# Band loads of 24 rows instead of 23 in a kernel of four attention layers

## The chip, the cores and the metric

The kernel runs on one core of a Trainium2 chip, as one program with one launch. The metric is the device time of that program in microseconds (us), the median of several runs. Times of single instructions come from one execution that the hardware profiler recorded.

## The reference, cut to what matters

Four layers of attention follow one another on 2048 tokens of 512 features with 32 heads of 16 features, each with a layer norm ahead and a residual behind:

```
x = A_x
x = x + _A_ref(_layernorm(x), A_wqkv, A_wo)   # dilated: token s sees s, s-2, ..., s-14
x = x + _B_ref(_layernorm(x), B_wqkv, B_wo)   # block: token s sees the last 256 tokens
x = x + _A_ref(_layernorm(x), A_wqkv, A_wo)
x = x + _B_ref(_layernorm(x), B_wqkv, B_wo)
```

The change is in layer A. There a query has eight keys, of its own parity (even or odd position): `logits = einsum("bhsd,bhswd->bhsw", q, kg) * scale`, a softmax over the eight, and `o = einsum("bhsw,bhswd->bhsd", attn, vg)`.

## The kernel before, in words

The sequence is cut into 8 chunks of 256 tokens, and the two pairs of layers run over them one after the other: for each pair of layers and each chunk first layer A (`layer_a`), then layer B (`layer_b`). That makes 16 chunks. All steps are given to a planner (`Plan`) as tasks with an engine, a cost and the values that they read and write. A table of numbers (`ORDER`) sets the order of each engine's tasks; the planner merges the five engines' rows by its costs, and so decides which buffers and PSUM banks a task gets. Steps of layer B of one chunk lie between steps of layer A of the next one. All but a few DMAs are issued by SP (SyncE), in the order of its row: an issue that must wait holds up all that stands behind it.

Layer A splits a chunk by parity into two halves of 128 tokens (`t` = 0 and 1). For each half TensorE (PE) computes scores in windows (L1171), ACT copies them out, and DMAs by way of DRAM bring the eight scores of each query into one row (`sd`, `l`). VectorE (DVE), ACT and GpSimd (POOL) make the softmax of them (L1212 to L1229), and L1223 writes the weights into `bands`, spread so that the two tokens of a pair stand side by side.

To weigh the values with them, PE needs the weights transposed: keys on the partitions. That is done by two DMAs through a DRAM tensor `ptd`, one for each half. `put` (L1256) writes `bands` with a stride that moves each query pair two rows down, so that a diagonal band arises; `ptd` is filled with zeros at the start, and `put` always writes the same places. `get` (L1263) reads the band back into `ptt`, an SBUF tile of 128 partitions that is set to zero once (L770), and of which there is only one. `get` issues four DMAs: `bb` = 0 and 1 are two groups of partitions from 0 and from 64, each with 39 keys (`WIN` = 39) for 32 queries; `e` = 0 and 1 are the first and the second eight query pairs of a group. One such DMA is a rectangle: so many rows (keys, on the partitions) by two blocks (`b2`) by 16 x 32 numbers of 4 bytes, which is 2 KB in one piece. The two rectangles of a group begin 16 rows apart and have 23 rows each: keys 0 to 22 and 16 to 38.

`window` (L1251) loads the values of the same keys from DRAM into `vs`: for each `bb` 39 rows by two blocks by 512 numbers, 2 KB in one piece too.

`mix` (L1280) then multiplies: two tasks of 64 matmuls for each half, each matmul with 39 keys in the contraction, alternately for `bb` = 0 and `bb` = 1. The matmuls of `bb` = 0 need the first pair of the four DMAs, those of `bb` = 1 the second. Since `ptt` exists once, the load of half 1 is issued only when the mix of half 0 is done. After the mix DVE picks the right one of two columns (`pick`, L1285), ACT and DVE split the result into two float16 parts (L1079, L1080), and PE multiplies it by the output weights (L1045, L1047, L1048).

Layer B has its scores in L1391 and L1542, with operands that DMAs bring by way of DRAM (`re`, `stk`), the row maxima in L1406, exponentials in L1552 and L1564, and the values in L1597. At its end the sums of the softmax go through `rc` and `scr` (L1660 to L1675) and are multiplied into the output `oc` (L1683).

Of the kernel before, what the change touches and what calls it, by code (L numbers as in the profile page):

```python
# [21 lines left out]
H = 32  # L22
# [5 lines left out]
WIN = 32 + HALO  # L28
# [628 lines left out]
def kernel(  # L657
# [10 lines left out]
    nc = tc.nc  # L668
# [9 lines left out]
    def buf(name, shape, dtype, tag, label, cap=None, group=0):  # L678
        p, n = pools[name]
        return Buf(p, cap or n, shape, dtype, tag, label, group)  # L680
# [43 lines left out]
    ptt = cst.tile([P, 2, 16, H, 2], F32, name="ptt")  # L724
# [391 lines left out]
    def layer_a(l, c):  # L1116
# [127 lines left out]
        for t in range(2):  # L1244
            vs = buf("pvs", [P, 2, D], F32, "vs", f"vs{l}_{c}_{t}")
            vvs = Val(vs)

            def window(t=t, vs=vs):
                x = vd[l][t]
                for bb in range(2):  # L1250
                    nc.sync.dma_start(vs.t[64 * bb : 64 * bb + WIN],  # L1251
                                      bass.AP(tensor=x.tensor, offset=x.offset + (c * P + 64 * bb) * D, ap=[[D, WIN], [32 * D, 2], [1, D]]))

            def put(t=t):
                x = ptd[t]
                nc.sync.dma_start(bass.AP(tensor=x.tensor, offset=x.offset, ap=[[130 * H, 64], [64 * H, WIN_], [1, 2 * H]]),  # L1256
                                  bands[64 * t : 64 * t + 64].rearrange("p k s u -> p k (s u)"))

            def get(t=t):
                x = ptd[t]  # L1260
                for bb in range(2):
                    for e in range(2):
                        nc.sync.dma_start(ptt[64 * bb + 16 * e : 64 * bb + 16 * e + WIN - 16, :, 8 * e : 8 * e + 8].rearrange("p a q s u -> p a (q s u)"),  # L1263
                                          bass.AP(tensor=x.tensor, offset=x.offset + (2 * bb * 65 * 32 + 16 * e * 65) * H, ap=[[64 * H, WIN - 16], [65 * H * 32, 2], [1, 16 * H]]))

            plan.add("SP", 0.8, window, r=[vvd[l, t, c], vvd[l, t, c - 1]], w=[vvs], size=560)
            plan.add("SP", 0.4, put, r=[ve], w=[vptd[t]], size=310)
            plan.add("SP", 1.65, get, r=[vptd[t]], w=[vptt], size=700)
            acc = Banks(psum, 2, [P, 2, 512])
            va, vpk = Val(acc), Val(acc)  # L1270
            accs.append(acc)
            vacc.append([vpk])

            def mix(m0, acc=acc, vs=vs):
                for m in range(m0, m0 + 2):
                    for b2 in range(2):
                        for r in range(4):
                            for bb in range(2):
                                k = slice(64 * bb, 64 * bb + WIN)
                                nc.tensor.matmul(acc.t[32 * r : 32 * r + 32, bb].rearrange("p (a x q u) -> p a x q u", a=2, q=16, u=2)[:, :, 2 * m + b2],  # L1280
                                                 vs.t[k, b2, 32 * (4 * m + r) : 32 * (4 * m + r) + 32], ptt[k, :, :, 16 * b2 + 4 * m + r],
                                                 start=True, stop=True, tile_position=(64 * bb, 32 * r))

            def pick(acc=acc):
                nc.vector.copy_predicated(acc.t[:, :, 0:C],  # L1285
                                          odd.bitcast(I16)[:, 0:1].unsqueeze(1).broadcast_to([P, 2, C]), acc.t[:, :, C:])

            for m0 in (0, 2):
                plan.add("PE", 0.85, lambda f=mix, m0=m0: f(m0), r=[vvs, vptt], w=[va], mode="V", act=0.5, rec=128)
            plan.add("DVE", 0.6, pick, r=[va, vodd], w=[vpk])  # L1290
# [472 lines left out]
```

## Time and profile before

| | |
|---|---|
| median of 3 runs | 1859.56 us (1859.2 to 1865.65) |
| the profiled execution | 1874.45 us, its span 1872.7 us |
| mean granted PE clock | 0.845 of full speed |
| DVE busy | 863.9 us (46%) |
| ACT busy | 825.9 us (44%) |
| POOL busy | 404.9 us (22%) |
| DMA | 183570 packets, 194.67 MB, mean 104 GB/s |

Busy time is the time in which an engine has an instruction under way; issuing a DMA and waiting do not count. A row of a group names line, engine, operation, output and inputs by the program's names, the count, then busy time and the mean of one in ns, then the engine's idle time just before these instructions and what ended most of it. In the timeline a row has start, length, engine (SPq is SP's queue of DMA issues), line and count, and in brackets the idle time ahead of it with what ended it. The table by stretches gives for each engine the busy time in a stretch and the count of instructions, then the granted PE clock, the share of time in which the core's 16 DMA engines were busy (their mean), and what they moved in GB/s.

### The profile page before, as it was taken

To read this page: it belongs to the slowest core of one execution; us is meant where nothing else is said; L and a number is where in the kernel's file an instruction comes from. 1 tells how busy PE (TensorE), PEld (TensorE's weight loads), DVE (VectorE), ACT (ScalarE), POOL (GpSimd) and SP (SyncE) were. 2 spreads that over 40 slices of the span, in tenths; PEclk is the share of its full clock that TensorE was granted. 3 is DMA by queue.
4 is the path that set the end of the run, shared out by engine and by line. 5 is a ranking of instruction groups with operands and counts; after the bars stand their busy time and mean duration, and the time that the engine had idled before them with its cause. 6 is when DMAs were issued, how large, how long until landed. Compare 5 with 4: busy or idle time off the path is not lost. (4 is left out here: it accounts for less than half of the span.)

```text
span 1872.7 us, 64356 instructions
## 1 busy us (share of the span) xinstructions
PE 1375.1 (73%) x28126; PEld 895.2 (48%) x28126; DVE 863.9 (46%) x1961; ACT 825.9 (44%) x1299; POOL 404.9 (22%) x856
## 2 busy tenths in 40 slices
PE   9657958678496784967949496784967678497687
PEld 7434636346263552735526263542735345263354
DVE  5413644453355453454624425453453444346366
ACT  7423526345263452634526162542635345253344
POOL 4120202122131211311313021321212222032112
PEclk9868979889797886988869797896978979788788
DMA  8753433626245254433414243344433454424232
GB/s 261 132 89 114 116 77 95 125 75 151 51 116 95 80 151 64 121 86 105 129 53 139 81 115 105 97 125 78 127 83 84 127 91 138 64 72 122 66 95 60
DMA packets 183570, 194.67 MB, mean 104 GB/s; under 512 B 91484, under 2 KB 121948, under 8 KB 183288
## 3 DMA queue, kind: packets, MB, share of 16 engines
q1 hardware_dynamic: 183032, 190.30, 40.7%
q8 instruction: 220, 3.60, 0.9%
q14 instruction: 62, 0.51, 0.1%
q10 hardware_dynamic: 256, 0.26, 0.1%
HBM read 93.59 MB, written 79.36 MB: 92 GB/s over the span
## 5 line engine op out<-in xcount | busy, mean ns | idle before, releaser
L1280 PE MATMUL banks<-ptt,vs 39*32 39x64 f32 x4096 | 77.8, 305 | 385.5 <-DMA ptt<-ptd 265.2
L1406 DVE TENSOR_REDUCE m<-banks 128x2 f32<-128x512 f32 x448 | 301.4, 688 | 8.2
L1552 ACT ACTIVATE p<-banks,sclB 128x896 f32<-128x896 f32 x224 | 220.7, 1005 | 84.2 <-PE banks L1542 73.5
L1280 PEld LDWEIGHTS banks<-ptt,vs 39*32 39x32 f32 x4096 | 63.7, 143 | 394.5 <-issue 367.7
L1410 DVE COPY_PREDICATED banks<-trm,banks 128x128 f32<-128x128 int16 x448 | 124.3, 291 | 170.1 <-PE banks L1391 163.0
L1079 ACT CAST oh<-banks 128x512 f16<-128x512 f32 x32 | 18.8, 587 | 415.4 <-DVE banks L1285 415.4
L1581 POOL TENSOR_SCALAR_AFFINE_SELECT p<-p 64x256 f32<-64x256 f32 x300 | 122.7, 431 | 347.0 <-ACT p L1552 333.1
L1285 DVE COPY_PREDICATED banks<-odd,banks 128x512 f32<-128x512 int16 x32 | 22.3, 696 | 377.1 <-PE banks L1280 377.0
L1581 POOL TENSOR_SCALAR_AFFINE_SELECT ps<-ps 64x256 f32<-64x256 f32 x292 | 115.8, 418 | 359.5 <-ACT ps L1564 354.4
L1391 PE MATMUL banks<-stk,stk 48*64 48x128 f16 (+3 forms) x3584 | 145.0, 253 | 45.6 <-DMA stk<-re 21.7
L1391 PEld LDWEIGHTS <-stk 48*64 48x64 f16 x3584 | 83.1, 113 | 123.6 <-issue 93.7
L1542 PE MATMUL banks<-stk,stk 64*64 64x192 f16 (+3 forms) x3584 | 124.4, 250 | 22.2 <-DVE m L1406 6.2
L1597 PE MATMUL banks<-p,v 64*32 64x256 f32 (+1 forms) x3584 | 131.5, 399 | 3.6 <-DVE p L1575 1.3
L1564 ACT ACTIVATE ps<-banks,sclB 128x768 f32<-128x768 f32 x112 | 100.1, 900 | 42.4 <-PE banks L1542 33.2
L1542 PEld LDWEIGHTS <-stk 64*64 64x64 f16 x3584 | 74.7, 113 | 74.7 <-issue 62.1
L1180 ACT COPY s<-banks 128x624 f32<-128x624 f32 x64 | 74.5, 1263 | 66.0 <-DMA sd<-s 42.9
L1312 DVE SCALAR_TENSOR_TENSOR el<-banks,eh 128x512 f16<-128x512 f32 x64 | 42.6, 688 | 114.5 <-ACT eh L1309 75.7
L1597 PEld LDWEIGHTS banks<-p,v 64*32 64x32 f32 x3584 | 68.5, 116 | 49.0 <-issue 26.3
L1683 POOL TENSOR_TENSOR oc<-oc,os 128x512 f32<-128x512 f32 x23 | 29.5, 1292 | 245.0 <-DMA os<-scr 75.1
L1614 ACT COPY os<-banks 128x256 f32<-128x256 f32 x112 | 41.4, 372 | 85.8 <-PE banks L1597 83.5
L1597 PE MATMUL banks<-ps,v 64*32 64x64 f32 (+1 forms) x3584 | 76.3, 264 | 3.7 <-issue 3.7
L1597 PEld LDWEIGHTS banks<-ps,v 64*32 64x32 f32 x3584 | 69.6, 114 | 16.0 <-issue 10.0
(216 smaller groups left out, 3245.1 us busy)
## 6 DMA issues: line engine op xcount, KB each, us to landing
stk<-re SPq DMA_DIRECT2D x256, 96.0 KB
sd<-s SPq DMA_DIRECT2D x128, 156.0 KB
re<-eh SPq DMA_DIRECT2D x128, 128.0 KB
ptt<-ptd SPq DMA_DIRECT2D x128, 92.0 KB
vs<-vd SPq DMA_DIRECT2D x64, 156.0 KB
vd<-ve SPq DMA_DIRECT2D x32, 256.0 KB
xm<-y SPq DMA_DIRECT2D x32, 256.0 KB
re<-el SPq DMA_DIRECT2D x64, 128.0 KB
```

Source lines behind the costliest of these rows:

```text
L1180: nc.scalar.copy(S_.t.rearrange("p k (s r) -> p r s k", r=4)[:, 2 * i : 2 * i + 2], pbs[i].t[:, :, 0 : 8 * WIN].rearrange("p r (s k) -> p ...
L1280: nc.tensor.matmul(acc.t[32 * r : 32 * r + 32, bb].rearrange("p (a x q u) -> p a x q u", a=2, q=16, u=2)[:, :, 2 * m + b2], vs.t[k, b2, 32 ...
L1312: nc.vector.scalar_tensor_tensor(e["l"].t[:, :, mp], ps[mp].t, QS, e["h"].t[:, :, mp], op0=ALU.mult, op1=ALU.subtract)
L1391: nc.tensor.matmul(o, lhs, k, start=True, stop=True, tile_position=(64 * par, 64 * h))
L1406: nc.vector.tensor_reduce(out=m.t[:, :, u, qb], in_=ps.t[:, :, 0 : 2 * P], op=ALU.max, axis=AX.X)
L1410: nc.vector.copy_predicated(t[:, :, 0:64], trm[:, 0].bitcast(I16).unsqueeze(1).broadcast_to([P, 2, 64]), t[:, :, C : C + 64])
L1542: nc.tensor.matmul(ps.t[64 * h : 64 * h + 64, par, at + x0 : at + x0 + q1 - q0], stk[hf, kt][r, col, k0 : k0 + 64], stk[hf, 0][r, col, q0: ...
L1552: nc.scalar.activation(big.t[:, 2 * i : 2 * i + 2], ps.t[:, :, 0:448], AF.Exp, scale=scl["B", 1])
L1564: nc.scalar.activation(small.t.rearrange("p (i m) x -> p m i x", i=2), ps.t[:, :, 0:384].rearrange("p m (i x) -> p m i x", i=2), AF.Exp, s ...
L1581: E.affine_select(out=v, in_=v, pattern=[[0, 4], [a, 64]], compare_op=op, fill=0.0, base=0, channel_multiplier=-a)
L1597: nc.tensor.matmul(acc.t[32 * mm : 32 * mm + 32, h, q0:q1], vv[r, blk, 17 * hd : 17 * hd + 32], x.t[r, mm, x0 : x0 + q1 - q0], start=begin ...
L1614: plan.add("ACT", 0.3, lambda acc=acc, some=some: nc.scalar.copy(some(), acc.t[:, 0, 0:C]), r=[vacc], w=[vhf])
```

## The change

The four rectangles of `get` have 24 rows instead of 23, and the two of a group begin 15 rows apart instead of 16: keys 0 to 23 and 15 to 38. The source address moves with it: the second rectangle begins 15 rows and eight pairs on, where it began 16 rows and eight pairs on. The keys that a group covers, 0 to 38, and the tile stay the same; the row added to each rectangle holds zeros of `ptd` outside the band. Tasks, costs, the order of every engine and the waits are the same as before; in SP's row 128 DMAs have another shape, 24x2x512 for 23x2x512.

```
             def get(t=t):
                 x = ptd[t]
                 for bb in range(2):
                     for e in range(2):
-                        nc.sync.dma_start(ptt[64 * bb + 16 * e : 64 * bb + 16 * e + WIN - 16, :, 8 * e : 8 * e + 8].rearrange("p a q s u -> p a (q s u)"),
-                                          bass.AP(tensor=x.tensor, offset=x.offset + (2 * bb * 65 * 32 + 16 * e * 65) * H, ap=[[64 * H, WIN - 16], [65 * H * 32, 2], [1, 16 * H]]))
+                        nc.sync.dma_start(ptt[64 * bb + 15 * e : 64 * bb + 15 * e + 24, :, 8 * e : 8 * e + 8].rearrange("p a q s u -> p a (q s u)"),
+                                          bass.AP(tensor=x.tensor, offset=x.offset + (2 * bb * 65 * 32 + 15 * e * 64 + 16 * e) * H, ap=[[64 * H, 24], [65 * H * 32, 2], [1, 16 * H]]))
```

## The prediction

> **What bounds the kernel now.** I read the page first, then the list of waits, then the timeline around one chunk's two band loads, and last the table by stretches for what the DMA engines do in them. The page has TensorE (PE) busy for 1375.1 of 1872.7 us, so it is without work for 497.6 us. The group table gives each group's idle time, and one group holds most of it:
>
> ```profile
> span 1872.7 us, 64356 instructions
> PE 1375.1 (73%) x28126; PEld 895.2 (48%) x28126; DVE 863.9 (46%) x1961; ACT 825.9 (44%) x1299; POOL 404.9 (22%) x856
> ...
> L1280 PE MATMUL banks<-ptt,vs 39*32 39x64 f32 x4096 | 77.8, 305 | 385.5 <-DMA ptt<-ptd 265.2
> ...
> ptt<-ptd SPq DMA_DIRECT2D x128, 92.0 KB
> ```
>
> L1280 is the mix of the dilated layer: 4096 matmuls are 32 mixes (16 chunks, two token halves) of 128. PE stands still for 385.5 us just before them, 12.0 us a mix; everywhere else it idles 497.6 - 385.5 = 112.1 us in all. The last row is the load that the mix waits for: 128 DMAs of 92.0 KB, four to a mix. The waits name the same cause, or none:
>
> ```profile
> PE banks L1280 <- DMA ptt<-ptd: 265.2, 46, 7.7
> PE banks L1280 <- issue: 84.7, 15, 7.7
> PE banks L1280 <- DMA vs<-vd: 23.0, 3, 12.2
> ```
>
> The 15 waits without a releaser have the same longest value, 7.7 us, as the 46 named ones, so I count them with these. The three on vs are the values' window; where its load stands behind the band load on SP, it is late because of that load. So I take all 385.5 us as the load's.
>
> Then one chunk in the middle. The timeline of SP's queue and that of PE (start, length, what; idle time before it in brackets):
>
> ```profile
> 813.32 5.74 SPq L1263 DMA_DIRECT2D ptt<-ptd  x4
> 819.10 5.69 SPq L1660 DMA_DIRECT2D rc<-os  x4
> ...
> 833.75 0.73 SPq L1251 DMA_DIRECT2D vs<-vd  x2
> 834.58 5.24 SPq L1263 DMA_DIRECT2D ptt<-ptd  x4
> 839.86 5.60 SPq L1665 DMA_DIRECT2D oc<-os  x4
> ```
>
> ```profile
> 824.20 0.39 PE L1280 MATMUL banks<-ptt,vs 39*32 39x64 f32 x2 [5.22 <-DMA ptt<-ptd]
> 831.68 2.04 PE L1280 MATMUL banks<-ptt,vs 39*32 39x64 f32 x126 [7.09 <-DMA ptt<-ptd]
> ...
> 844.86 0.27 PE L1280 MATMUL banks<-ptt,vs 39*32 39x64 f32 x2 [4.03 <-DMA ptt<-ptd]
> ...
> 852.50 2.03 PE L1280 MATMUL banks<-ptt,vs 39*32 39x64 f32 x126 [7.38 <-DMA ptt<-ptd]
> ```
>
> The second load is issued from 834.58. Its first pair of DMAs (partitions 0 to 38) lets two matmuls go at 844.86, 10.3 us later; the second pair lets the other 126 go at 852.50, 17.9 us after the issue. The pairs are 7.64 us apart, and a pair is 2 x 92.0 KB = 188,416 bytes: 24.7 GB/s. The stretches show why so slow:
>
> ```profile
> core 0: us, PE busy (x) PEld busy (x) DVE busy (x) ACT busy (x) POOL busy (x), PEclk, DMA share, GB/s
> 819.50:824.00 4.50, 0.00 (x0) 0.00 (x0) 0.00 (x0) 0.29 (x1) 0.00 (x0) 0.78 0.08 28
> 824.50:831.00 6.50, 0.09 (x1) 0.00 (x0) 0.00 (x0) 0.00 (x0) 0.00 (x0) 0.50 0.33 99
> 834.50:836.00 1.50, 1.50 (x10) 1.16 (x9) 1.44 (x3) 0.57 (x1) 0.00 (x0) 0.62 0.66 199
> 837.00:840.50 3.50, 3.50 (x35) 1.77 (x33) 2.41 (x5) 0.36 (x1) 0.00 (x0) 1.00 0.07 26
> ...
> 845.50:852.40 6.90, 0.00 (x0) 0.00 (x0) 0.00 (x0) 0.00 (x0) 0.00 (x0) 0.53 0.18 45
> ```
>
> From 837.0 to 840.5 little but the band load is under way, and the 16 DMA engines are busy for a share of 0.07 at 26 GB/s. One engine of 16 is a share of 0.0625: the load runs through one engine, its four DMAs one behind the other (4 x 94,208 bytes at 26 GB/s is 14.5 us). Just before, from 834.5 to 836.0, the window loads issued at 833.75 move at 199 GB/s and a share of 0.66. They read the same way, rows of 2 KB in two blocks, and differ in having 39 rows rather than 23. So it is not the row's size, nor HBM, that confines the band load. In 824.5 to 831.0 and 845.5 to 852.4 nothing computes on any engine: the wait is hidden by nothing.
>
> **The change, part by part.** It makes the 128 DMAs of L1263 24 rows instead of 23. No instruction is added, removed or moved on any engine, and no wait is new.
>
> The load's length. The nearest row for a load of the same form that spreads is the window's 199 GB/s: 24 x 2 x 2048 = 98,304 bytes take 0.49 us instead of 3.6 (94,208 at 26 GB/s), four 2.0 us instead of 14.5. The four issues and the time from issue to landing come on top; for these the nearest rows are four unblocked issues on SP, and in the chain of waits a DMA of 144 KB from its issue to what it releases:
>
> ```profile
> 1708.48 2.50 SPq L1660 DMA_DIRECT2D rc<-os  x4
> ```
>
> ```profile
> 1716.68 2.79 DMA ptd<-bands
> ```
>
> The first pair then lands 0.6 + 2.8 = 3.4 us after the load's first issue, the last DMA 1.9 + 2.8 = 4.7 us after it, or 5.3 where it queues a little. When does PE come to the mix? In the rows above at 824.20 - 5.22 = 818.98, which is 5.7 us after the issue at 813.32, and at 844.86 - 4.03 = 840.83, 6.25 us after the issue at 834.58. There nothing of the wait is left. Elsewhere PE comes sooner:
>
> ```profile
> 935.14 2.42 SPq L1263 DMA_DIRECT2D ptt<-ptd  x4
> ```
>
> ```profile
> 945.13 0.39 PE L1280 MATMUL banks<-ptt,vs 39*32 39x64 f32 x2 [6.98 <-DMA ptt<-ptd]
> ```
>
> That is 938.15, 3.0 us after the issue, and about 2 us would stay. I take 1.0 us left per mix, between 0 and 3: 32 us of the 385.5.
>
> [...]
>
> The clock. After a wait of this length PE works at half clock for a while. These are PE's starts after the first mix, then a few later:
>
> ```profile
> 833.83 0.42 PE L1026 MATMUL banks<-xl,wA0h 128*128 128x256 f16 x1
> 834.05 0.42 PE L1027 MATMUL banks<-xh,wA0l 128*128 128x256 f16 x1
> 834.26 0.42 PE L1025 MATMUL banks<-xh,wA1h 128*128 128x256 f16 x1
> ...
> 835.81 0.27 PE L1027 MATMUL banks<-xh,wA1l 128*128 128x256 f16 x1
> 835.92 0.27 PE L1025 MATMUL banks<-xh,wA1h 128*128 128x256 f16 x1
> ```
>
> The same matmuls start every 0.21 us and then every 0.11. Here nine of them, from 833.64 to 835.54, lose 0.95 us. After another mix it lasts longer:
>
> ```profile
> 1162.50:1169.50 7.00, 6.51 (x77) 3.20 (x77) 5.01 (x12) 4.19 (x5) 1.56 (x4) 0.50 0.54 113
> ```
>
> Seven microseconds at 0.50 with PE busy for 6.51 lose up to 3.3. Without the long waits this loss goes too: between 1 and 3 us a mix, and I take 1.5, which is nearer to the row of the first: 48 us.
>
> What comes late instead. Work of other engines that lies in the waits today must find another place. In the stretches above DVE, ACT and POOL do nothing or 0.29 us. A stretch before another mix has more:
>
> ```profile
> 1603.00:1616.00 13.00, 0.39 (x2) 0.18 (x2) 1.88 (x4) 0.00 (x0) 1.47 (x4) 0.66 0.84 35
> ```
>
> DVE's 1.88 us there is the upper end, 32 x 1.88 = 60 us if PE had to wait for all of it; the lower end is 0, and even below it, since the load also holds up what SP issues behind it (rc<-os took 5.69 us to issue where 2.50 is usual, oc<-os 5.60), and DVE waits for one of these:
>
> ```profile
> DVE rc L1669 <- DMA rc<-os: 39.5, 3, 14.5
> ```
>
> I take 30 us of new waits. The two rows added cost 4 KB a DMA in 94 KB; at the window's rate that is 0.02 us a DMA.
>
> The sum, against the profiled execution (1874.45 us with what lies around its span): 1874.45 - 385.5 + 32 - 48 + 30 = 1502.95. That execution stands above the median of the runs by 1874.45 / 1859.56 = 1.008. So 1503 / 1.008 = 1491, rounded **1490 us**.
>
> **The rivals.**
>
> *Slower: the load's time goes by its bytes, whatever its rows.* If something other than the row count confines it to one engine (the overlapping of the two rectangles, the place in DRAM), each DMA carries two packets of 2 KB more at 26 GB/s: 0.16 us, 0.63 for four, 20 us over 32 mixes, 1859.56 + 20 = 1880 us. It decides when the share in such a stretch stays near 0.07. For it: the trace has no load of 24 rows. Against it: the window load, of the same form from the same kind of tensor, is seven times as fast. [...] Chance 0.03; that the compiled load is cut as before, so that nothing changes (1860 us), 0.01.
>
> *Two engines instead of many.* The load would take 7.5 us instead of 14.5 and each mix would win some 7 us, and the half clock would stay: 1859.56 - 32 x 7 = 1636 us. Against it again the window's 0.66. Chance 0.04.
>
> *Another wait takes half of it back.* The chain from a mix to the next layer's output (rc, reciprocal, scr, os, the product at L1683) runs beside the second load today. If PE comes to its product earlier than that chain, it could wait 6 us a chunk and mix: 1490 + 32 x 6 = 1682 us. For it: PE's order is fixed, so one late product stops all behind it. Against it: that chain is late today because its DMAs are issued behind the band load. Chance 0.08.
>
> **How the numbers follow.** The forecast has a chance of 0.84. Its own ends: with nothing left of the wait, 2 us of clock a mix and no new waits, 1874.45 - 385.5 - 64 = 1425, by 1.008 about 1414; with 3 us left a mix, 1 us of clock and 60 us new, 1874.45 - 385.5 + 96 - 32 + 60 = 1613, about 1600. The low end needs three favourable ends at once, and I stop at 1425. 1425 to 1600 leaves out the rivals (0.16) and little of the forecast's own. All but the first rival are faster by far more than 0.5% (about what a measurement of this kernel can tell from no change): faster 0.96, same 0.01, slower 0.03.
>
> **What would show it.** Right: in the changed profile the idle time before L1280 falls from 385.5 to below 100 us, PE's busy share rises from 73% to about 90%, the mean clock from 0.845 to above 0.9, and in the stretch behind a load the DMA share is no longer 0.07 for ten microseconds; SP's four issues of L1263 take about 2.5 us instead of 5. Wrong: if the waits of L1280 on ptt stay at 7 us each, the row count was not the cause; if they go and PE's idle time grows by as much before other lines (L1047 and L1048 behind the product, or L1391 behind stk), the third rival holds; if the clock stays near 0.845 with the waits gone, the 48 us are wrong.

## The result, and the profile after

The changed kernel takes 1471.07 us (median of 4 runs, 1469.52 to 1476.47), the kernel before 1862.61 us on the same chip (1859.2 to 1878.7): a ratio of 0.789, with a 95% interval from 0.7838 to 0.7941. 1490 us were forecast. The profiled execution of the changed kernel took 1476.47 us, its span 1474.8 us, at a mean granted PE clock of 0.949.

The page of the changed kernel, with the rows that answer to those shown of before:

```profile
span 1474.8 us, 64356 instructions
...
PE 1324.0 (90%) x28126; PEld 866.4 (59%) x28126; DVE 866.2 (59%) x1961; ACT 825.8 (56%) x1299; POOL 405.7 (28%) x856
...
L1391 PE MATMUL banks<-stk,stk 48*64 48x128 f16 (+3 forms) x3584 | 144.1, 249 | 51.1 <-DMA stk<-re 26.0
...
L1280 PE MATMUL banks<-ptt,vs 39*32 39x64 f32 x4096 | 59.6, 237 | 24.6 <-issue 12.4
...
ptt<-ptd SPq DMA_DIRECT2D x128, 96.0 KB
```

PE's idle time before the mix fell from 385.5 to 24.6 us. The instructions are the same in number, and DVE, ACT and POOL are busy for the same time as before; only the share of the span has grown. The groups that now wait most on PE are others, L1391 first, but with little more than before (51.1 us, before 45.6 us).

SP's queue around the same chunk as in the prediction, in the changed kernel:

```profile
641.37 2.92 SPq L1263 DMA_DIRECT2D ptt<-ptd  x4
644.33 2.51 SPq L1660 DMA_DIRECT2D rc<-os  x4
...
650.62 0.91 SPq L1251 DMA_DIRECT2D vs<-vd  x2
651.63 1.56 SPq L1263 DMA_DIRECT2D ptt<-ptd  x4
653.23 2.46 SPq L1665 DMA_DIRECT2D oc<-os  x4
```

And PE's mixes there:

```profile
647.26 1.64 PE L1280 MATMUL banks<-ptt,vs 39*32 39x64 f32 x128
...
655.87 0.27 PE L1280 MATMUL banks<-ptt,vs 39*32 39x64 f32 x2 [0.81 <-DVE y L1092]
656.87 1.32 PE L1280 MATMUL banks<-ptt,vs 39*32 39x64 f32 x107 [0.73 <-DMA ptt<-ptd]
```

The first mix runs through without a wait. The second load is issued at 651.63; its first matmul goes 4.2 us later (before: 10.3), and the 0.81 us of wait ahead of it are put down to DVE, no longer to the load. Of the other 126, 107 follow 5.2 us after the issue (before: 17.9), where a wait of 0.73 us on the load ends. The issues behind the loads (rc, oc) take 2.5 us, where before they took 5.69 and 5.60: with the slow load, SP's issues behind it took longer too.

The table by stretches of the changed kernel, across the second load of that chunk:

```profile
core 0: us, PE busy (x) PEld busy (x) DVE busy (x) ACT busy (x) POOL busy (x), PEclk, DMA share, GB/s
...
653.50:655.00 1.50, 1.50 (x8) 0.49 (x5) 1.45 (x3) 0.00 (x0) 0.00 (x0) 1.00 0.69 190
654.50:656.00 1.50, 0.69 (x5) 0.20 (x3) 1.26 (x3) 0.23 (x1) 0.00 (x0) 1.00 0.81 219
```

A share of 0.69 to 0.81 at 190 to 219 GB/s stands where 0.07 and 26 GB/s stood behind the same load (837.00 to 840.50 in the prediction's table). Some of this is other traffic, so the share is not the load's alone.

From all rows of L1263 and L1280 in the two traces one can work out where in a chunk the time went, as means over 16 chunks:

| stretch | before | after |
|---|---|---|
| issue of the first load to the end of its mix | 20.1 us | 7.6 us |
| end of that mix to the issue of the second load | 1.2 us | 2.1 us |
| issue of the second load to the end of its mix | 20.6 us | 8.2 us |
| end of that mix to the next chunk's first load (15) | 68.5 us | 67.6 us |

The first and the third stretch lose 12.4 to 12.5 us a chunk each, 398 us over 16 chunks; the spans differ by 1872.7 - 1474.8 = 397.9 us. The second grows by 0.9 us and the fourth shrinks by as much: all else cancels.

### The profile page after: what moved, and what is told of

Same layout as the page of the kernel before. It is cut to its first block, busy times and chain, and to the rows that moved or that the text cites. A ratio compares the mean times of both kernels' runs of the same rounds, so it can differ in the third digit from the quotient of the medians.

```text
span 1474.8 us, 64356 instructions
## 1 busy us (share of the span) xinstructions
PE 1324.0 (90%) x28126; PEld 866.4 (59%) x28126; DVE 866.2 (59%) x1961; ACT 825.8 (56%) x1299; POOL 405.7 (28%) x856
## 5 line engine op out<-in xcount | busy, mean ns | idle before, releaser
L1391 PE MATMUL banks<-stk,stk 48*64 48x128 f16 (+3 forms) x3584 | 144.1, 249 | 51.1 <-DMA stk<-re 26.0
L1391 PEld LDWEIGHTS <-stk 48*64 48x64 f16 x3584 | 82.0, 111 | 131.8 <-issue 97.3
L1597 PE MATMUL banks<-p,v 64*32 64x256 f32 (+1 forms) x3584 | 120.7, 371 | 6.1 <-issue 3.0
L1597 PEld LDWEIGHTS banks<-p,v 64*32 64x32 f32 x3584 | 64.9, 110 | 45.6 <-issue 24.5
L1611 DVE TENSOR_TENSOR os<-os,banks 128x256 f32<-128x256 f32 x104 | 42.4, 416 | 70.1 <-ACT os L1614 60.9
L1280 PE MATMUL banks<-ptt,vs 39*32 39x64 f32 x4096 | 59.6, 237 | 24.6 <-issue 12.4
L1597 PEld LDWEIGHTS banks<-ps,v 64*32 64x32 f32 x3584 | 66.0, 108 | 15.2 <-issue 11.3
L1026 PE MATMUL banks<-xl,wA0h 128*128 128x256 f16 x256 | 72.1, 282 | 2.8 <-DMA xl<-xn 2.8
L1025 PE MATMUL banks<-xh,wA0h 128*128 128x256 f16 x256 | 72.3, 282 | 0.3 <-ACT v L1343 0.2
L1027 PE MATMUL banks<-xh,wA0l 128*128 128x256 f16 x256 | 72.1, 282 | 0.0
```

Source lines behind the costliest of these rows:

```text
L1025: nc.tensor.matmul(ps[mp].t[:, i], wh, xh, start=k == 0, stop=False)
L1026: nc.tensor.matmul(ps[mp].t[:, i], wh, xl, start=False, stop=False)
L1027: nc.tensor.matmul(ps[mp].t[:, i], wl, xh, start=False, stop=k == 3)
L1391: nc.tensor.matmul(o, lhs, k, start=True, stop=True, tile_position=(64 * par, 64 * h))
L1597: nc.tensor.matmul(acc.t[32 * mm : 32 * mm + 32, h, q0:q1], vv[r, blk, 17 * hd : 17 * hd + 32], x.t[r, mm, x0 : x0 + q1 - q0], start=begin ...
```

## The experiments

The theory: such a load is spread over as many engines as the largest divisor of its row count up to 16, and for 23 that is one; the time is that of one engine's queue, and nothing hides it. The traces show the two ends of this, a share of 0.07 behind a load of 23 rows and of 0.69 to 0.81 behind one of 24; that the divisor sets the count was the author's assumption when these runs were planned, and how it fared stands under the rivals below. For 24 rows it gives twelve engines, an estimated 98,304 / 12 = 8,192 bytes each and, at the 26 GB/s of the 23-row load, 0.32 us a DMA or 1.3 us for four. The main rivals: the new geometry (start and overlap of the rectangles) made the difference, or the parity or size of the count. All of the following change only L1260 to L1264, unless something else is said. All ratios are to the kernel before on the same chip.

**29 rows**, a prime number:

```
-  ptt[64 * bb + 15 * e : 64 * bb + 15 * e + 24, ...]   ap=[[64 * H, 24], ...]
+  ptt[64 * bb + 10 * e : 64 * bb + 10 * e + 29, ...]   ap=[[64 * H, 29], ...]
```

> Rectangles of 29 rows (the second one 10 rows below the first); everything else as in the changed kernel, and the same result is computed. Theory (the number of engines is the largest divisor of the row count up to 16): 29 has none but 1, so one engine again; a DMA is 118,784 bytes, at 26 GB/s 4.6 us, four 18.3 instead of the 14.5 of 23 rows, 3.8 us more on each of 32 loads that nothing hides: about 1862 + 122 = 1984 us, L1280 idle above 480 us. Rival (the new start of the second rectangle, or more rows as such, freed the load): about 1471 us, L1280 idle near 25 us.

Measured: 1994.01 us against 1855.53, ratio 1.0725 (1.0652 to 1.0797). Its page, and the stretch behind a load:

```profile
L1282 PE MATMUL banks<-ptt,vs 39*32 39x64 f32 x4096 | 78.1, 306 | 498.3 <-DMA ptt<-ptd 371.6
```

```profile
886.00:892.00 6.00, 4.12 (x38) 2.04 (x35) 3.44 (x7) 0.81 (x2) 0.00 (x0) 1.00 0.07 26
```

The share is 0.07 at 26 GB/s as with 23 rows, about that of one engine of 16 (0.0625), and the wait is 113 us longer than with 23 rows. The time rises by 138 us, where 122 were expected. More rows and another start of the second rectangle do not free the load by themselves. With the two pieces below, which keep the old places and are fast, the geometry is out as the cause.

**25 rows**, odd, and divisible by 5:

```
-  ptt[64 * bb + 15 * e : 64 * bb + 15 * e + 24, ...]   ap=[[64 * H, 24], ...]
+  ptt[64 * bb + 14 * e : 64 * bb + 14 * e + 25, ...]   ap=[[64 * H, 25], ...]
```

> Rectangles of 25 rows. Theory (largest divisor up to 16): five engines, 102,400 / 5 = 20,480 bytes each, 0.8 us a DMA at 26 GB/s, four 3.2 us instead of 1.3 with twelve; of these 1.9 us a part is hidden, so 1471 to 1520 us. Rival (odd counts, or counts that are no multiple of 8, go through one engine): four DMAs 15.8 us, about 1862 + 32 x 1.3 = 1902 us.

Measured: 1503.79 us, ratio 0.8074 (0.803 to 0.8118). In its page:

```profile
L1282 PE MATMUL banks<-ptt,vs 39*32 39x64 f32 x4096 | 61.0, 244 | 41.9 <-DMA ptt<-ptd 18.4
```

An odd count is fast, and the time lies in the theory's range of 1471 to 1520 us, so parity is out. It is slower than 24 rows (ratios of 0.789 and 0.7934), as the theory has it of five engines, and the wait lies between that of 24 rows and that of one engine, near the first: 41.9 us.

**32 rows**, the second rectangle 7 rows below the first; and the same again beside the changed kernel, since the first comparison was across chips:

```
-  ptt[64 * bb + 15 * e : 64 * bb + 15 * e + 24, ...]   ap=[[64 * H, 24], ...]
+  ptt[64 * bb + 7 * e : 64 * bb + 7 * e + 32, ...]     ap=[[64 * H, 32], ...]
```

> Rectangles of 32 rows. Theory: 16 engines, 131,072 / 16 = 8,192 bytes each, the same 0.32 us a DMA as with 24 rows on twelve: 1471 us within 0.5%, if PE's wait is no longer set by the load's bytes. Rival (the bytes of the load set the time, now spread): a third more bytes, at the window's 199 GB/s 0.16 us a DMA, 0.66 us a load, 1471 + 21 = 1492 us.

> The changed kernel again, beside 32 rows on the same chip. Theory (both counts spread, bytes no longer on the path): the two agree within 0.5%. Rival (a third more bytes cost 12 us): 24 rows are 0.8% faster.

> 32 rows again, beside 24 rows on the same chip. Theory: within 0.5% of 24 rows. Rival: 0.8% slower, 12 us.

Measured: at first 1482.96 us, ratio 0.7984 (0.7941 to 0.8027); side by side 1491.21 us (0.8024, 0.7996 to 0.8051) for 32 rows and 1478.17 us (0.7934, 0.7914 to 0.7955) for 24. So 32 rows are 0.9% slower, 13 us, and the theory's "within 0.5%" is wrong here: by the theory an engine carries 8,192 bytes a DMA with 32 rows on 16 engines as with 24 rows on twelve, and still the load is later. In the two profiles of the side-by-side runs (the first is that of 24 rows) the mix's wait differs by as much:

```profile
L1280 PE MATMUL banks<-ptt,vs 39*32 39x64 f32 x4096 | 59.3, 239 | 24.8 <-issue 13.2
```

```profile
L1282 PE MATMUL banks<-ptt,vs 39*32 39x64 f32 x4096 | 60.7, 242 | 37.3 <-DMA ptt<-ptd 19.3
```

In the profile of the earlier run of 32 rows the wait was 24.5 us, so this part of it is not steady. An issue on SP takes 425 ns (median of 128) instead of 369, four a load: 7 us over 32 loads. The times at which the DMAs land stand in the traces too. Side by side, the last DMA of a load lands on average 5.39 us after the load's first issue with 32 rows and 5.00 with 24, so 0.39 us later, 12.5 us over 32 loads, as much as the wait grows. The four issues together make 0.25 us of this (2.07 against 1.82); whether the other 0.14 us are the bytes on the way or the landing stays open. In the earlier run the last landing was at 5.23 us, against 5.10 in the changed kernel.

**The old rectangles in two pieces**: 23 rows at the old places, as 12 and 11 (shown against the kernel before):

```
+  for a, n in ((0, 12), (12, 11)):
-      ptt[64 * bb + 16 * e : 64 * bb + 16 * e + 23, ...]
+      ptt[64 * bb + 16 * e + a : 64 * bb + 16 * e + a + n, ...]
```

> The rectangles of before, 23 rows at the old places, but each loaded as two DMAs of 12 and 11 rows: the same bytes to the same places, eight DMAs a load instead of four. Theory: 12 and 11 engines, so the one-engine queue is gone; four more issues at 0.4 to 0.6 us put the last landing 1.6 to 2.4 us later than with 24 rows: 1475 to 1540 us. Rival (the old geometry, not the count, confines the load): 1862 us or more.

Measured: 1517.45 us, ratio 0.8163 (0.8123 to 0.8203). The same bytes go from the same places to the same places, and 88% of the gain is there (338 of 384 us, with 1855.53 x 0.793 = 1471 for 24 rows). So neither the places nor the bytes confined the load. That smaller DMAs made the difference is ruled out by 24 and 32 rows, whose DMAs are larger and fast; the count of rows in a DMA is left. Part of what the two pieces lose against 24 rows is the issue of eight DMAs (the row is from its SP queue): the last one lands on average 5.71 us after the load's first issue, 0.6 us later than in the changed kernel, some 20 us over 32 loads. The rest of the 46 us stays open.

```profile
671.71 4.38 SPq L1265 DMA_DIRECT2D ptt<-ptd  x8
```

**One DMA a group**, 39 rows and all pairs:

```
-  for e in range(2):
-      ptt[64 * bb + 15 * e : 64 * bb + 15 * e + 24, :, 8 * e : 8 * e + 8]   ap=[[64 * H, 24], ..., [1, 16 * H]]
+  ptt[64 * bb : 64 * bb + 39]                                               ap=[[64 * H, 39], ..., [1, 32 * H]]
```

> One DMA per group instead of two: all 39 rows with all sixteen pairs, pieces of 4 KB, so two DMAs a load instead of four, and 639 KB instead of 393 KB. Theory: 39 rows go through 13 engines, 24,576 bytes each, 0.95 us a DMA at 26 GB/s; the two issues saved (0.8 us) make up for it: 1471 us within 1%. Rival (bytes decide once the load is spread, as 32 rows, 12 us above 24, might mean): 246 KB more at 199 GB/s are 1.2 us a load, 1471 + 40 = 1511 us.

Measured: 1511.74 us, ratio 0.8112 (0.8072 to 0.8151). The theory's "within 1%" is missed and the rival's 1511 met: with the load spread, the bytes that carry zeros still cost here, and two issues fewer do not make up for them. The last DMA of a load lands 6.8 us after its first issue, against 5.1 in the changed kernel, and PE idles for 53.2 us before the mix (L1279 in this kernel).

**24 rows in one half of each chunk**, `24 if t == 0 else 23`:

> 24 rows for the first token half of each chunk, 23 for the second. Theory (each load's wait is its own): half of the change's 392 us, so 1862 - 196 = 1666 us, between 1640 and 1690; L1280 idle about 200 us. Rival (the second load, which is issued only behind the first mix, takes over what the first one wins, or the first alone holds all up): above 1750 or below 1580 us.

Measured: 1679.0 us, ratio 0.9018 (0.8998 to 0.9038): 185 us of the change's 391, and 211.7 us of wait left before the mix. The loads do not trade waits with each other; each has its own.

**Eight rows**:

```
-  ptt[64 * bb + 15 * e : 64 * bb + 15 * e + 24, ...]   ap=[[64 * H, 24], ...]
+  ptt[64 * bb + 16 * e : 64 * bb + 16 * e + 8, ...]    ap=[[64 * H, 8], ...]
```

> Rectangles of only 8 rows (at the old starts), so a third of the load's bytes, on eight engines, with four issues as before; most of the band's rows are left out, so the result is not the reference's. Theory (with 24 rows the load's bytes are off the path, what is left is its issue and its landing): at most the 24.6 us that L1280 still idles can go, 1450 to 1471 us. Rival (bytes still set the time, by the 12 us that 32 rows cost over 24): 16 rows fewer give 24 us or more, below 1447 us.

Measured: 1465.66 us, ratio 0.7875 (0.7854 to 0.7897). A third of the bytes gains 3 to 11 us over 24 rows (ratios of 0.789 and 0.7934 in the two comparisons). In its page:

```profile
L1282 PE MATMUL banks<-ptt,vs 39*32 39x64 f32 x4096 | 56.2, 236 | 17.1 <-issue 14.8
```

The waits named for the load are nearly gone, and 17.1 us stay. The last landing comes at 3.7 us instead of 5.1, some 45 us sooner over 32 loads, and the time gains no more than 11: most of the 24-row load is off the path.

**PE kept at full clock without the change.** In the kernel of 23 rows, matmuls that nobody uses (the function `warm`) fill PE's two waits. The first try put them into the half of the mix that the code adds first:

```
+                def warm(n):
+                    for _ in range(n):
+                        nc.tensor.matmul(acc.t[:, 1, 0 : 2 * P], v[:, 0:P], v, start=True, stop=True)
+                if m0 == 0:
+                    warm(24)
...
+                                if m0 == 0 and m == b2 == r == 0 and bb == 1:
+                                    warm(44)
```

> The kernel of before (23 rows) with matmuls that nobody uses in PE's waits: 24 ahead of each mix, 44 between its first matmul and its second, 256 columns each, 0.11 us at full clock, written where the mix writes afterwards. Theory (PE's 51 us less busy time in the changed kernel are the half clock that follows a long wait): PE is at full clock when the load lands, and the mix and the matmuls after it take 32 to 64 us less over 32 loads: about 1800 to 1835 us, mean clock above 0.93, while L1280's waits stay. Rival (the clock plays no part): 1860 us or more, since the fillers only add work.

Measured: 2032.39 us, ratio 1.0923 (1.0891 to 1.0955). This tells nothing of the clock. In the chunk around 916 us, the order table runs the half with `m0` = 2 first; there the fillers came behind the wait, as plain work of 4.2 us for 24, and overwrote what the other half had written (that part of the mix is lost in this kernel). The second try puts them into whichever half runs first (`ahead = not begun` in place of `m0 == 0`):

> As the last experiment with unused matmuls in the 23-row kernel, but now in the half of the mix that really runs first: 24 ahead of its first matmul, 44 between its first and its second, where PE waits for the load's two pairs. Theory (the half clock after a long wait makes up PE's 51 us more busy time): the fillers lie in the waits, PE is at full clock when the last pair lands, and 25 to 64 us go: 1800 to 1838 us, mean clock above 0.93, the idle time before L1280's matmuls now partly filled. Rival (the clock plays no part): 1860 us or more.

Measured: 1857.09 us (10 runs) against 1862.38, ratio 0.9978 (0.9963 to 0.9992): 4 to 5 us, and neither theory nor rival. Its page, its group rows, and one wait filled as meant:

```profile
PE 1600.0 (86%) x30302; PEld 1090.9 (59%) x30302; DVE 862.9 (47%) x1961; ACT 825.6 (45%) x1299; POOL 405.4 (22%) x856
```

```profile
L1281 PE MATMUL banks<-idf 128*128 128x256 f16 x2176 | 282.1, 295 | 0.5 <-DVE m L1420 0.2
...
L1294 PE MATMUL banks<-ptt,vs 39*32 39x64 f32 x4096 | 62.9, 242 | 137.2 <-DMA ptt<-ptd 71.2 <-issue 46.9 <-DMA vs<-vd 16.5
```

```profile
816.11 2.78 PE L1281 MATMUL banks<-idf 128*128 128x256 f16 x24
...
821.49 0.27 PE L1294 MATMUL banks<-ptt,vs 39*32 39x64 f32 x2 [2.60 <-DMA ptt<-ptd]
821.69 4.98 PE L1281 MATMUL banks<-idf 128*128 128x256 f16 x44
829.03 1.76 PE L1294 MATMUL banks<-ptt,vs 39*32 39x64 f32 x126 [2.36 <-DMA ptt<-ptd]
```

Without its fillers PE is busy for 1600.0 - 282.1 = 1317.9 us, 57 us less than before and about what the changed kernel has (1324.0), at a mean clock of 0.936. So the slow clock after the waits (0.845 in the mean before, 0.50 in the stretch from 1162.5 us) does explain PE's longer busy time. But the wait, fillers included, is 137.2 + 282.1 = 419.3 us where it was 385.5, 34 us more. The load's last DMA still lands 17.7 us after the first issue (17.9 before), so where PE comes to the mix sooner, it waits longer; how much of the 34 us is fillers that did not fit into a wait stays open. Between the two profiled executions the time falls by 22 us (1874.45 to 1852.36), but the execution of before that was profiled is slower than all 17 runs of before that stand beside this kernel (1855.89 to 1871.75). The medians differ by 5 us, and these decide: with the load slow, most of the 57 us that the clock gave PE was lost again in the wait.

## Why the prediction was right, step by step

The account stands as it was put: 23 rows at the share of about one engine (0.07), nothing to hide the wait, and nothing serious late behind it. That 24 rows would spread was the author's assumption; no trace of before has a load of 24 rows, and the changed kernel's has (0.69 to 0.81). The terms, each of the profiled executions:

| term | forecast | measured |
|---|---|---|
| PE's wait before the mix, left over | 32 us of 385.5 | 24.6 us |
| clock, as PE's busy time | -48 us | 1324.0 - 1375.1 = -51.1 us |
| new waits elsewhere on PE | +30 us | 112.1 to 126.2 us: +14.1 us |
| sum | -371.5 us | -360.9 - 51.1 + 14.1 = -397.9 us |

*What is left of the wait.* The load's last landing was put at 4.7 to 5.3 us after the issue; the row quoted above has 5.2, and the mean of all 32 loads is 5.1 (before 17.9). The four issues on SP take 1.56 to 2.92 us there, forecast 2.5.

*The clock.* Its size was right, on PE's account. As a gain of its own it was not: the filled waits show that with the load as it was, 57 us of PE's busy time brought 4 to 5 us by the medians (22 between the two profiled executions). It is the removal of the load that turns it into time. The forecast added it where that was allowed, because the load went with it.

*New waits.* The forecast's 30 us were twice too many. The product at L1683, the third rival, did not become late: its chain begins behind the load on SP and came forward with it (rc and oc issue in 2.5 us), as the argument against that rival said. PE's idle time before the matmuls behind that product (L1047 on `wB3h` and `oh`) is 7.4 us in all, before 5.1.

*What was luck.* The wait left (0 to 3 us a mix) and the clock (1 to 3 us a mix) were picked inside wide ranges; that they came out 7 and 3 us off is in part luck. The new waits were the term most off, by 16 us.

*The rivals.* That bytes decide whatever the rows is ruled out by 24 rows and by the two pieces of 23. That only two engines would carry the load, which would have taken some 1636 us, is ruled out by the time and by the 24.6 us of wait that are left. The author's assumption, the largest divisor up to 16, agrees with every count tried: 23 and 29 are slow at a share of 0.07, and 24, 25, 32, 39, 12 and 11, and 8 are fast (ratios from 0.7875 to 0.8163).

The traces say more of the counts. They hold every rise of the semaphores by which the DMAs report. All band DMAs with the same rows have the same number of rises:

| rows of a DMA | rises of its semaphore | a load's last landing, mean us after its first issue |
|---|---|---|
| 23 | 2 | 17.9 |
| 29 | 2 | 21.6 |
| 25 | 6 | 6.5 |
| 8 | 9 | 3.7 |
| 12 and 11 | 13 and 12 | 5.7 |
| 24 | 13 | 5.1 |
| 39 | 14 | 6.8 |
| 32 | 16 | 5.2 |

With all counts but 32 one rise comes early, 0.2 us (median) after the issue has ended; the next comes 1.2 us after that end at the earliest. With 32 rows there is no such early rise: the first comes after 2.0 us (median). Without the early one, the rises are 1, 1, 5, 8, 12 and 11, 12, 13 and 16: each time the largest divisor up to 16 of that row count. That every such rise is one engine's share is the author's reading; the share of 0.07 agrees with it for 23 and 29 rows. Which of the 16 engines they are the traces do not tell, and no other count was run for this load.

*From the profiled time to the median.* I divided by 1.008, the ratio of before; after the change the two stand at 1476.47 / 1471.07 = 1.004. That is 6 us in the other direction, and part of why 1490 is only 19 us off where the sum is 26 off.

## What to carry to other kernels

If one load shows a DMA share near 1/16 and a few tens of GB/s while a load of the same form moves several times as fast (here a share of 0.07 and 26 GB/s beside 0.66 and 199 GB/s), look at its row count before anything else. A row of zeros more, or the load in two pieces, was worth about a fifth of the time here (ratios of 0.789 and 0.8163), and the row count was worth more than the bytes it added, up to a point: 24 rows (0.789 and 0.7934) beat 25 (0.8074), 32 (0.7984 and 0.8024) and 39 (0.8112). PE's slow clock after the waits was a consequence of them here (0.845 in the mean with them, 0.949 without), and curing it alone (0.936) brought 4 to 5 of 1862 us.

## What the runs showed of the hardware

The load with a share of 0.07 also held up its neighbours: SP's four issues behind it took 5.6 to 5.7 us instead of 2.5. The semaphore of a DMA rose 2 times for 23 rows, 13 for 24, 16 for 32; less the early rise of all counts but 32, that is the largest divisor up to 16 for each count of the table above. More rises did not mean a shorter time: 32 rows were 13 us slower than 24, side by side, and their loads landed 0.39 us later. And fillers that raised PE's mean clock from 0.845 to 0.936 moved the median by 4 to 5 us only.
